# Attention and two MLPs on one core: more q/k and V-half buffers, V read once per batch, W1o staged in its own tile, W1i's low halves on VectorE

## The chip, the cores and the metric

One core of one Trainium2 chip. The time is the device time of one execution in microseconds (us). Engines are called as in the profile: PE is TensorE, DVE is VectorE, ACT is ScalarE, POOL is GpSimd, SP is SyncE, which issues all DMAs here.

## The reference

Inputs are q, k, v of shape (4 batches, 8 heads, 576 positions, 64), and four weight matrices: W1i and W2i (512 x 2048), W1o and W2o (2048 x 512). All are float32, except that the kernel receives the weights as 64-bit values seen as pairs of 32-bit words.

```
q_rot, k_rot = rotate(q), rotate(k)
scores = scale * q_rot @ k_rot.T
attn = exp(scores - max) / (sum + 1e-9)
x = (attn @ v) as (2304 tokens, 512)
x = gelu_sigmoid(x @ W1i) @ W1o
out = elu(x @ W2i) @ W2o
```

## The kernel before, in words

**Precision.** Every large matrix product is done in two 16-bit halves: an operand is scaled, rounded to a high half (f16), and the remainder is kept as a low half. Three products (high-high, high-low, low-high) are added in PSUM. So each operand costs one operation for its high half (mostly ACT) and one for its low half (mostly DVE).

**Blocks and groups.** The 2304 tokens are cut into nine blocks: batch 0 into three of 128, 192 and 256 tokens, each later batch into two of 320 and 256. The eight heads are taken as four pairs. The attention of one pair in one block is called a group here. `s_units` does it for each query chunk: score matmuls (L702), maximum (L707, DVE), exponential (L711, ACT), reciprocal of the sum (L718, L722), high and low half of the weights (L727 or L729, L733), and a DMA transpose into a buffer of the pool `et` (L742). A full chunk has two tiles of 128x576, one per head; the 64 tail positions of both heads share one tile. `av_unit` then does attention times V for the group (L770) and splits the result into an `x` buffer (L773, L777). A block with its four `x` buffers complete can go through the first MLP: `first_mlp` (L821 and L858 on PE, L824 to L839 on ACT and DVE). Blocks 0 and 1 share one activation buffer `ghl`; from block 2 on, the MLP of a block starts when the one before has ended.

**What must come first.** `prep` (L570) loads q and k of a pair into a buffer `R`, rotates them on DVE (L582, L586, L590) with a buffer `T`, turns them on PE (L595) and stores them in a buffer `qkT` (L600) that stays taken until the pair's last score matmul of the batch. `v_prep` (L628) loads V per pair with four DMAs (L638, L640) into one of four `V` buffers, takes its largest absolute value (L644 or L646), and when the batch's scale is known splits it into halves in `v16` (L665, L669), of which shifted copies are made by three DMAs (L674 to L676).

**Weights.** `Weight` (L375) loads W1i and W1o in 16 chunks of 512 KB each (L406) into raw buffers: for W1i four places in `ghl` (`G`), for W1o two buffers of their own (`Go`). A chunk is brought to float32 by L413 and L420 (ACT or DVE), L427 and L432 (DVE only), and measured by four small matmuls (L446). When all 16 are through and the scale is known, each chunk is split in place into its high half (L489 or L491) and its low half. The low half is normally DVE's (L495). For W1i's first 12 chunks (`pe_w1i=12`) it is PE's instead: two float32 products with a scaled unit matrix (L503) minus one with the high half (L504), and a copy out of PSUM (L509 on ACT or L511 on DVE). The scaled unit matrix (L479) and the negative one (`minus`, L562) are made on POOL.

**The order.** Nothing is issued in program order. `Plan.run` is a list scheduler that runs when the kernel is built: every operation has a cost for each engine that may take it, a key (lower goes first, from the table `TUNE`), the operations it comes after, and the buffers it needs from pools whose sizes stand in `BUFS`. An operation without a free buffer is passed over for the next by key. The order in which the plan takes operations is the order of each engine's instructions, SP's DMA issues among them; on the chip each engine then works through its list in that order.

```
        o1 = op({"pe": ...}, mm, qk_ready[b, hp], key - TUNE["s"], need=[("s", x) for x in hS], use=[hX])
...
            trs.append(op(*cost, lambda e, a=a: tr(e, a), [o7] + trs[:1], key + a - TUNE["tr"], need=[("et", hT)] if fst else (), use=[hEl[a]] + ([] if fst else [hT])))
```

So a group takes its `et` buffer, of which there are two, at its first transpose and gives it back after its L770.

Of the kernel before, what the change touches and what calls it, by code (L numbers as in the profile page):

```python
# [20 lines left out]
    s=2, av=1, m=3, E=3, Ehl=3, et=2, qkT=2, R=1, V=4, T=2, v16=3, x=9, t=3, y=1, R2=3, yhl=1, o=3,  # L21
)
TUNE = dict(
    pe_w1i=12, pe_w1o=0, tab=-297.6168609712772, f_dve=2174.208136010006, f_act=81.41105488268754, f_pool=1052.0627577352195,
    w1i2=233.92485834008724, w1o2=-15.505291206809591, dlat=823.3988909607715, kt=-377.2719573514129, slack=1000000000.0,
    w1i=-242.99841865529547, w1i_s=3.8061508400859974, w1o=2.969689623870087, w1o_s=0.2720231588088968, prep0_s=3.8536381936457946,
    prep0=17.464678152527306, prep=-308.1411248258243, va0=-34.247727670237225, va=-64.95846168300157, vs=243.43590834219214,
    tiny=52.0380520808221, av=136.85433893694528, ex=-71.59782834058082, mx=198.562005486859, s=130.46174549696988, tr=52.58804387596749,
    w2i2=-139.37012827254537, w2o2=-97.97140032540149,
# [190 lines left out]
def kernel(  # L220
# [88 lines left out]
    buf("V", ap_, [P, 640], F32, BUFS["V"])  # L309
    buf("T", ap_, [P, 9, 2, D], F32, BUFS["T"])  # L310
    buf("v16", ap_, [P, 2, 5, 2, D], F16, BUFS["v16"])
    buf("vsh", ap_, [P, 4, 2, D], F16, BUFS["v16"])
# [22 lines left out]
    def across(am, hM, after, key, add=False, use=()):  # L335
# [19 lines left out]
        o = op({"pe": 300.0}, turn, list(after) + [ready_c], key, need=[("m", hM)], use=use)  # L355
# [19 lines left out]
    class Weight:  # L375
        def __init__(self, tile_fn, src, wide, tag, rbuf, key, after=()):
# [20 lines left out]
            for i, c in enumerate(seq):  # L397
                kc = key(i)

                def load(e, c=c):  # L400
                    if wide:
                        kk, f = c // 4, c % 4
                        s = src[kk * P:kk * P + P, 1024 * f:1024 * f + 1024]
                    else:
                        s = src[c * P:c * P + P, :]
                    nc.sync.dma_start(out=take((tag, c))[:, 0:1024].bitcast(I32), in_=s)  # L406
# [28 lines left out]
                ld = op(*dma_in(P * 4096), load, after, kc, need=[(rbuf, h)])  # L435
                self.loads.append(ld)
                ox = op({"act": c_act(512) + 70, "dve": c_dve(512, 2)}, cx, [ld], kc, use=[h], port=True)
# [3 lines left out]
                if by_pe:  # L441
                    def norm(e, c=c, i=i):
                        y = take((tag, c))[:, 0:1024].bitcast(BF16).rearrange("p (f w) -> p f w", w=4)[:, :, 3]
# [32 lines left out]
            if TUNE.get("pe_" + tag, 0):  # L476
                def scaled_eye(e):
                    self.eye = ap_.tile([P, P], F32, name=tag + "_eye")
                    ENG[e].tensor_scalar(out=self.eye, in0=eye, scalar1=self.sc["s"], scalar2=1.0, op0=ALU.mult, op1=ALU.mult)  # L479

                oe = op({"dve": 200, "pool": 360}, scaled_eye, [so, ready_c], key(15), port=True)
            self.ready = [None] * 16
            free = {}
            for i, c in enumerate(seq):
# [13 lines left out]
                if i < TUNE.get("pe_" + tag, 0):  # L498
                    hm = (tag, "lo", c)

                    def mm(e, c=c, i=i, hm=hm):
                        ps = take(hm)
# [3 lines left out]
                    def lo_(e, c=c, hm=hm):  # L506
                        l = self.h[:, self.at[c], 512:1024]
                        if e == "act":
                            nc.scalar.activation(out=l, in_=take(hm), func=AF.Copy)  # L509
                        else:  # L510
                            nc.vector.tensor_copy(l, take(hm))  # L511

                    o3 = op({"pe": 1500.0}, mm, [o2, oe], ks, need=[("m", hm)])
                    self.ready[c] = free[i + SP] = op({"act": c_act(512, True), "dve": c_dve(512)}, lo_, [o3], ks, use=[hm])
                    continue
# [27 lines left out]
    minus = ap_.tile([P, P], F16, name="minus")  # L543
# [6 lines left out]
    buf("Go", ap_, [P, 1024], F32, 2)  # L550
# [10 lines left out]
    def consts(e):  # L561
        nc.gpsimd.tensor_scalar(out=minus, in0=eye, scalar1=-1.0, scalar2=1.0, op0=ALU.mult, op1=ALU.mult)  # L562

    lit = op({"pool": 100}, light, key=-200.0)
    begin = op({"dma": 480}, 1600.0, start, key=TUNE["tab"])
    ready_c = op({"pool": 400}, consts, [begin], key=TUNE["tab"])


    def prep(b, hp):
# [41 lines left out]
        for g in range(3):  # L611
            t = op({"pe": 360.0}, lambda e, g=g: turn(e, g), [r3, ready_c, t], key, need=[("m", hX + (g,))] + ([] if g else [("qkT", hX)]), use=[hT] + ([hX] if g else []))
# [12 lines left out]
    v_loaded = {}  # L625
    def v_view(b, hp):
        return take(("vs", b, hp)).rearrange("p (a d) -> p a d", d=D)

    def v_prep(b):
        ka = first_u[fb[b], 0] - TUNE["va" if b else "va0"]  # L630
        ams = []
        for hp in range(NP):
            h, h0 = ("vs", b, hp), 2 * hp

            def ld_(e, h=h, h0=h0, hp=hp):
                t = v_view(b, hp)
                for a in range(2):
                    nc.sync.dma_start(out=t[:, a:8:2, 0:D], in_=v[b, h0 + a, 0:512, :].rearrange("(p j) d -> p j d", j=4))  # L638
                for a in range(2):
                    nc.sync.dma_start(out=t[64 * a:64 * a + 64, 8:10, 0:D], in_=v[b, h0:h0 + 2, 512:S, :].rearrange("h p d -> p h d"))  # L640

            def am(e, h=h, hp=hp):
                if e == "act":
                    nc.scalar.activation(out=junk.rearrange("p (a d) -> p a d", d=D), in_=v_view(b, hp)[:, :, 0:D], func=AF.Abs, saturate=False, accum_out=v_am[b % 2][:, hp:hp + 1])  # L644
                else:
                    nc.vector.tensor_reduce(out=v_am[b % 2][:, hp:hp + 1], in_=v_view(b, hp)[:, :, 0:D], axis=AX.XY, op=ALU.max, apply_absolute_value=True)  # L646

            ld = v_loaded[b, hp] = op(*dma_in(330e3, 4), ld_, [], ka + hp, need=[("V", h)])
# [11 lines left out]
        for hp in range(NP):  # L660
            ks = last_u[fb[b], hp] - TUNE["vs"]
            h, hv, hw = ("vs", b, hp), ("v16", b, hp), ("vsh", b, hp)

            def hi(e, hp=hp, hv=hv):
                nc.scalar.activation(out=take(hv)[:, 0].rearrange("p j h d -> p (j h) d"), in_=v_view(b, hp)[:, :, 0:D], func=AF.Copy, scale=sc["s"])  # L665

            def lo(e, hp=hp, hv=hv):
                X = take(hv).rearrange("p w j h d -> p w (j h) d")
                nc.vector.scalar_tensor_tensor(out=X[:, 1], in0=v_view(b, hp)[:, :, 0:D], scalar=sc["s"], in1=X[:, 0], op0=ALU.mult, op1=ALU.subtract)  # L669
            o1 = op({"act": c_act(640, ptr=1)}, hi, [so], ks, need=[("v16", hv)], use=[h])  # L670
# [617 lines left out]
```

## Time and profile before

| | |
|---|---|
| median of 3 runs | 1058.03 us (1056.73 to 1059.0) |
| the profiled execution | 1058.17 us, span 1056.4 us |
| PE busy | 978.3 us (93%) |
| DVE busy | 858.2 us (81%) |
| ACT busy | 608.0 us (58%) |
| mean granted PE clock | 0.982 |
| PE busy, tenths, by fortieths of the span | 2578689999999999999999999999989999999997 |

The span runs from the first to the last instruction. The last line shows PE nearly always busy except in the first six fortieths, about 26 us each. A busy PE need not be at its full rate: the granted clock tells at which of two levels it ran (1.0 is 2.4 GHz, 0.5 is 1.2 GHz).

### The profile page before, as it was taken

The numbers are of one execution on the slowest core, as the hardware profiler recorded it, in microseconds if no ns is written. First come the engines' busy times: TensorE is split into PE (matmuls) and PEld (weight loads), VectorE is DVE, ScalarE is ACT, GpSimd is POOL, SyncE is SP. The second block draws the span as 40 slices with busy tenths as digits, with TensorE's granted clock in tenths as the row PEclk, the third lists the DMA queues.
The fourth block names the chain that finished last, engine by engine and source line by source line (L and its number), as shares of the span: only waits on it lengthen the run. The fifth ranks groups of instructions, "written<-read, shape, count | busy, mean of one in ns | idle before, by whom it ended". The sixth has DMA issues, their size and how long they took to land. (4 is left out here: it accounts for less than half of the span.)

```text
span 1056.4 us, 20058 instructions
## 1 busy us (share of the span) xinstructions
PE 978.3 (93%) x7790; PEld 686.8 (65%) x7790; DVE 858.2 (81%) x1688; ACT 608.0 (58%) x1167; POOL 1.7 (0%) x8
## 2 busy tenths in 40 slices
PE   2578689999999999999999999999989999999997
PEld 1234468877766667866678778744435855855886
DVE  6988899789788779786574979899999579579474
ACT  4767789547577658566563648476355145145151
POOL 0000000000000000000000000000000000000000
PEclk9989889999999999999999999999999999999999
DMA  8889966677767786672773442620000100100100
GB/s 305 235 191 196 210 119 110 125 132 141 132 145 124 128 131 128 108 126 24 130 127 119 156 143 89 199 81 1 20 21 20 46 16 3 63 16 9 38 16 20
DMA packets 233086, 109.45 MB, mean 104 GB/s; under 512 B 203040, under 2 KB 222112, under 8 KB 232992
## 3 DMA queue, kind: packets, MB, share of 16 engines
q1 hardware_dynamic: 232992, 108.18, 47.0%
q8 instruction: 61, 1.00, 0.4%
q14 instruction: 33, 0.27, 0.1%
HBM read 53.61 MB, written 9.44 MB: 60 GB/s over the span
## 5 line engine op out<-in xcount | busy, mean ns | idle before, releaser
L821 PE MATMUL m<-x,wi 128*128 128x256 f16 (+3 forms) x1728 | 198.0, 273 | 0.5 <-DVE t L827 0.5
L858 PE MATMUL m<-ghl,wo 128*128 128x256 f16 (+3 forms) x1728 | 197.5, 273 | 0.0
L1053 PE MATMUL m<-yhl,w2i 128*128 128x512 f16 (+1 forms) x960 | 190.2, 360 | 4.4 <-DVE e L1064 4.2
L858 PEld LDWEIGHTS <-wo 128*128 128x128 f16 x1728 | 155.9, 98 | 41.5 <-issue 12.4
L821 PEld LDWEIGHTS <-wi 128*128 128x128 f16 x1728 | 155.7, 98 | 41.8 <-issue 12.5
L1053 PEld LDWEIGHTS <-w2i 128*128 128x128 f16 x960 | 94.3, 98 | 98.2 <-issue 7.4
L733 DVE SCALAR_TENSOR_TENSOR Ehl<-E,st,Ehl 128x576 f16<-128x576 f32 x144 | 116.3, 811 | 26.7 <-ACT Ehl L727 25.7
L711 ACT ACTIVATE E<-s,st 128x576 f32<-128x576 f32 x144 | 106.1, 738 | 49.3 <-DVE st L707 28.9
L702 PE MATMUL s<-qkT 64*128 64x288 f32 (+1 forms) x640 | 116.1, 466 | 10.0 <-ACT E L711 9.9
L727 ACT ACTIVATE Ehl<-E,st 128x576 f16<-128x576 f32 x117 | 89.3, 769 | 54.1 <-DMA et<-Ehl 38.3
L707 DVE TENSOR_REDUCE st<-s 128x1 f32<-128x576 f32 x144 | 107.0, 750 | 11.6 <-PE s L702 11.3
L1056 ACT ACTIVATE e<-m,y_c 128x512 f32<-128x512 f32 (+1 forms) x80 | 50.7, 638 | 72.9 <-issue 48.7
L702 PEld LDWEIGHTS s<-qkT 64*128 64x128 f32 (+1 forms) x640 | 60.3, 191 | 42.1 <-ACT E L711 17.2
L1129 PEld LDWEIGHTS <-g 128*128 128x128 f16 x714 | 70.3, 99 | 9.5 <-issue 0.7
L824 ACT ACTIVATE t<-m,hsc 128x320 f32<-128x320 f32 (+3 forms) x96 | 55.4, 577 | 25.1 <-PE m L821 23.2
L1149 DVE SCALAR_TENSOR_TENSOR x<-z,eo,x 128x256 f32<-128x256 f32 x49 | 23.3, 482 | 49.6 <-PE z L1129 49.3
L827 DVE SCALAR_TENSOR_TENSOR t<-t,m 128x320 f32<-128x320 f32 (+3 forms) x96 | 52.4, 547 | 10.6 <-ACT t L824 10.2
L836 ACT ACTIVATE ghl<-t 128x320 f16<-128x320 f32 (+3 forms) x96 | 49.8, 520 | 15.6 <-DVE t L827 15.1
L1129 PE MATMUL z<-wo,g 128*128 128x256 f16 x504 | 58.0, 277 | 0.0
L1064 DVE SCALAR_TENSOR_TENSOR e<-m,y_c,e 128x512 f32<-128x512 f32 (+1 forms) x80 | 55.0, 690 | 0.4
L839 DVE SCALAR_TENSOR_TENSOR ghl<-t,ghl 128x320 f16<-128x320 f32 (+3 forms) x96 | 52.5, 549 | 3.3 <-ACT ghl L836 3.0
L770 PE MATMUL av<-et,v 128*64 128x256 f16 (+3 forms) x720 | 50.9, 290 | 3.5 <-DMA et<-Ehl 3.5
(164 smaller groups left out, 1241.0 us busy)
## 6 DMA issues: line engine op xcount, KB each, us to landing
ghl<-in_moe_w_in_dram SPq DMA_DIRECT2D x16, 512.0 KB, 6.7
Go<-in_moe_w_out_dram SPq DMA_DIRECT2D x16, 512.0 KB, 4.3
R<-in_moe_w_in_dram SPq DMA_DIRECT2D x16, 512.0 KB, 4.1
R<-in_moe_w_out_dram SPq DMA_DIRECT2D x16, 512.0 KB, 3.7
R<-in_k_dram SPq DMA_DIRECT2D x16, 256.0 KB, 2.9
R<-in_q_dram SPq DMA_DIRECT2D x16, 256.0 KB, 3.6
V<-in_v_dram SPq DMA_DIRECT2D x32, 128.0 KB, 2.9
R<-y_d SPq DMA_DIRECT2D x8, 512.0 KB, 4.3
```

The source lines that it names most:

```text
L702: nc.tensor.matmul(o, X[r, t:t + (TAIL if h is None else P)], X[r, NS * w:NS * w + NS], start=True, stop=True)
L707: nc.vector.tensor_reduce(out=st["t"][:, a:a + 1], in_=take(hS[a])[:, :, 0:NS], axis=AX.XY, op=ALU.max, negate=True)
L711: nc.scalar.activation(out=take(hE[a]).rearrange("p (c f) -> p c f", c=2), in_=take(hS[a])[:, :, 0:NS], func=AF.Exp, bias=t[:, a:a + 1], s ...
L727: nc.scalar.activation(out=X16[:, 0:S], in_=take(hE[a]), func=AF.Copy, scale=r)
L733: nc.vector.scalar_tensor_tensor(out=X16[:, S:2 * S], in0=E, scalar=r, in1=X16[:, 0:S], op0=ALU.mult, op1=ALU.subtract)
L821: nc.tensor.matmul(ps, W1i.lhs(kk, u, wl), x[:, xl, 0:N], start=kk == 0 and i == 0, stop=kk == KD - 1 and i == 2)
L824: nc.scalar.activation(out=flat(ht), in_=flat(hM), func=AF.Tanh, scale=hsc[b][:, 1:2])
L839: nc.vector.scalar_tensor_tensor(out=g_of(gl), in0=t_of(), scalar=DOWN / 2, in1=g_of(gh), op0=ALU.mult, op1=ALU.subtract)
L858: nc.tensor.matmul(ps[:, 0:N], W1o.lhs(f, d, wl), (gh, gl)[xl][:, f, g0:g0 + N], start=f == 0 and i == 0, stop=f == KF - 1 and i == 2)
L1053: nc.tensor.matmul(ps[:, 0:n], W2i.lhs(kk, u, wl), Y[:, xl, kk, 0:n], start=kk == 0 and i == 0, stop=kk == KD - 1 and i == 2)
L1064: nc.vector.scalar_tensor_tensor(out=t[:, 0:n], in0=take(hM)[:, 0:n], scalar=st["c"][:, 0:1], in1=t[:, 0:n], op0=ALU.mult, op1=ALU.max)
L1129: nc.tensor.matmul(ps, AT[A](p, gi, P * tt), BT[B](p, wl), start=p == 0 and i == 0, stop=p == 7 and i == 2)
```

## The change

- Pools: `qkT` 2 to 4, `R` 1 to 2, `T` 2 to 1, `v16` (with `vsh`) 3 to 4, `x` 9 to 10, `V` from four buffers of one pair to one buffer of the whole batch.
- V of a batch is loaded by three DMAs and kept by head, so each pair's half is one contiguous piece; the halves and the shifted copies follow that layout.
- W1o's raw chunks lie in the part of W1o's own tile that is not yet written: chunks 0 to 7 in four places, 8 to 11 in two, 12 and 13 in one, 14 and 15 in the buffers `R`. Where a chunk's result falls on a place that held another raw chunk, it waits for that one (`over`).
- The PE way of making low halves is taken out, with `minus` and the scaled unit matrix: all W1i low halves are made by L495.
- A group's `et` buffer is taken by its first score matmul instead of its first transpose; the group's later score matmuls come after the first.
- All keys in `TUNE` are other numbers.

```
 BUFS = dict(
-    s=2, av=1, m=3, E=3, Ehl=3, et=2, qkT=2, R=1, V=4, T=2, v16=3, x=9, t=3, y=1, R2=3, yhl=1, o=3,
+    s=2, av=1, m=3, E=3, Ehl=3, et=2, qkT=4, R=2, V=1, T=1, v16=4, x=10, t=3, y=1, R2=3, yhl=1, o=3,
 )
...
-    pe_w1i=12, pe_w1o=0, tab=-297.6168609712772, f_dve=2174.208136010006, f_act=81.41105488268754, f_pool=1052.0627577352195,
...
+    tab=-755.3495038560459, f_dve=3717.3294571158176, f_act=658.9801078794787, f_pool=2518.1827925442094, w1i2=409.947966353374,
+    w1o2=-286.50084735922803, dlat=823.3988909607715, kt=40.753958365620065, slack=1000000000.0, w1i=-646.8295163812928,
...
+            stage = rbuf if callable(rbuf) else lambda c: rbuf
+            if callable(rbuf):
+                for k in range(4):
+                    buf(f"{tag}{k}", lambda i, k=k: self.t[:, 9 + 2 * k:11 + 2 * k, :].rearrange("p a b -> p (a b)"), None, None, 1)
...
+                over = []
+                if callable(rbuf) and c > 7:
+                    x = (4, 5, 10, 13)[(c - 8) // 2]
+                    over = [conv[x], am_ops[x]]
+                ox = op({"act": c_act(512) + 70, "dve": c_dve(512, 2)}, cx, [ld] + over, kc, use=[h], port=True)
...
-                if i < TUNE.get("pe_" + tag, 0):
-                    hm = (tag, "lo", c)
...
-                        nc.tensor.matmul(ps, self.eye, self.t[:, i + SP, :], start=True, stop=False)
-                        nc.tensor.matmul(ps, minus, self.h[:, self.at[c], 0:512], start=False, stop=True)
...
+        def ld_(e):
+            t = take(h)
+            nc.sync.dma_start(out=t[:, :, 0:4, :], in_=v[b, :, 0:512, :].rearrange("h (p j) d -> p h j d", j=4))
+            for a in range(2):
+                nc.sync.dma_start(out=t[64 * a:64 * a + 64, :, 4, :], in_=v[b, :, 512:S, :].rearrange("h p d -> p h d"))
+
+        ld = op(*dma_in(1311e3, 3), ld_, [], ka, need=[("V", h)])
...
-                nc.sync.dma_start(out=Y[0:64], in_=X[64:P, 0, 0:4])
-                nc.sync.dma_start(out=Y[64:P], in_=X[0:64, 0, 1:5])
-                nc.sync.dma_start(out=X[64:P, :, 4], in_=X[0:64, :, 0])
+                nc.sync.dma_start(out=Y[0:64], in_=X[64:P, 0, :, 0:4])
+                nc.sync.dma_start(out=Y[64:P], in_=X[0:64, 0, :, 1:5])
+                nc.sync.dma_start(out=X[64:P, :, :, 4], in_=X[0:64, :, :, 0])
...
-        o1 = op({"pe": 1260.0 if h is not None else 800.0}, mm, qk_ready[b, hp], key - TUNE["s"], need=[("s", x) for x in hS], use=[hX])
+        o1 = op({"pe": 1260.0 if h is not None else 800.0}, mm, qk_ready[b, hp] + first[:1], key - TUNE["s"], need=[("s", x) for x in hS] + ([("et", hT)] if i == first_u[n, hp] else []), use=[hX] + ([] if i == first_u[n, hp] else [hT]))
+        first.append(o1)
...
-    W1o = Weight(lambda: per.tile([P, 16 + SP, 512], F32, tag="wo", name="wo"), w1_out, False, "w1o", "Go", lambda c: TUNE["w1o"] + TUNE["w1o_s"] * c)
+    W1o = Weight(lambda: per.tile([P, 16 + SP, 512], F32, tag="wo", name="wo"), w1_out, False, "w1o", lambda c: f"w1o{c % 4 if c < 8 else 2 + c % 2 if c < 12 else 3}" if c < 14 else "R", lambda c: TUNE["w1o"] + TUNE["w1o_s"] * c)
```

## Rows read from the trace of the kernel before

**Rows 1.** Stretches of the span: span part, busy time (instructions) of each engine.
```profile
core 0: us, PE busy (x) PEld busy (x) DVE busy (x) ACT busy (x) POOL busy (x), PEclk, DMA share, GB/s
7.00:144.00 137.00, 86.31 (x610) 50.31 (x610) 123.61 (x243) 98.42 (x195) 0.93 (x1) 0.90 0.91 221
144.00:231.00 87.00, 82.50 (x1036) 71.42 (x1036) 77.95 (x147) 62.35 (x138) 0.00 (x0) 1.00 0.65 114
231.00:303.00 72.00, 71.22 (x648) 54.71 (x646) 61.69 (x118) 47.20 (x99) 0.00 (x0) 1.00 0.79 148
480.00:567.00 87.00, 86.59 (x761) 64.64 (x760) 53.05 (x101) 49.28 (x100) 0.00 (x0) 1.00 0.47 79
```

**Rows 2.** Timeline of PE: start, duration, instructions.
```profile
68.95 1.28 PE L770 MATMUL av<-et,v 128*64 128x128 f16 x20
...
144.14 1.81 PE L821 MATMUL m<-x,wi 128*128 128x128 f16 x24
...
183.66 1.24 PE L702 MATMUL s<-qkT 64*128 64x288 f32 x8
...
185.92 1.28 PE L770 MATMUL av<-et,v 128*64 128x256 f16 x20
...
230.86 4.10 PE L821 MATMUL m<-x,wi 128*128 128x256 f16 x36
```

**Rows 3.** Groups of PE's instructions from 0 to 231 us, by form.
```profile
L702 PE MATMUL s<-qkT 64*128 64x288 f32 x184 | 42.1, 532 | 3.9 <-ACT E L711 3.9
L503 PE MATMUL m<-wi,w1i_eye 128*128 128x512 f32 x24 | 14.4, 685 | 1.1 <-ACT qkT L600 1.1
L595 PE MATMUL m<-eye,T 128*128 128x128 f32 x63 | 12.7, 334 | 7.7 <-DVE T L590 4.7 <-ACT qkT L600 1.4 <-DVE t L827 1.1
L702 PE MATMUL s<-qkT 64*64 64x288 f32 x56 | 11.3, 536 | 5.7 <-ACT E L711 5.6
L770 PE MATMUL av<-et,v 128*64 128x256 f16 x100 | 7.2, 287 | 1.5 <-DMA et<-Ehl 1.5
L504 PE MATMUL m<-wi,minus 128*128 128x512 f16 x12 | 5.0, 412 | 5.3 <-ACT wi L489 5.3
L770 PE MATMUL av<-et,v 128*64 128x320 f16 x20 | 1.5, 301 | 0.0
```

**Rows 4.** Groups of DVE's instructions from 0 to 231 us.
```profile
L733 DVE SCALAR_TENSOR_TENSOR Ehl<-E,st,Ehl 128x576 f16<-128x576 f32 x49 | 39.5, 809 | 5.2 <-ACT Ehl L727 5.1
L707 DVE TENSOR_REDUCE st<-s 128x1 f32<-128x576 f32 x52 | 38.9, 748 | 3.2 <-PE s L702 3.1
L582 DVE TENSOR_TENSOR T<-R,tab 128x576 f32<-128x576 f32 x16 | 12.0, 750 | 1.0 <-DMA R<-in_q_dram 0.7 <-issue 0.2
L495 DVE SCALAR_TENSOR_TENSOR wo<-wo,w1o_s 128x512 f16<-128x512 f32 x16 | 11.8, 736 | 0.0
L590 DVE TENSOR_TENSOR T<-T,R 128x1152 f32<-128x1152 f32 x8 | 10.8, 1349 | 0.0
L586 DVE TENSOR_TENSOR R<-R,tab 128x1152 f32<-128x1152 f32 x8 | 10.8, 1345 | 0.0
L669 DVE SCALAR_TENSOR_TENSOR v<-V,v_s,v 128x640 f16<-128x640 f32 x8 | 6.8, 876 | 0.0
```

**Rows 5.** Timeline of DVE: two L733 in a row.
```profile
66.53 1.54 DVE L733 SCALAR_TENSOR_TENSOR Ehl<-E,st,Ehl 128x576 f16<-128x576 f32 x2
```

**Rows 6.** Waits of PE from 0 to 250 us: total, times, longest.
```profile
PE m L446 <- DVE ghl L427: 21.2, 11, 8.1
```

**Rows 7.** Timeline of SP's queue: two DMA issues for V.
```profile
43.30 2.61 SPq L640 DMA_DIRECT2D V<-in_v_dram  x2
```

**Rows 8.** DMA issues of the whole span: count, size, median us to landing.
```profile
Go<-in_moe_w_out_dram SPq DMA_DIRECT2D x16, 512.0 KB, 4.3
V<-in_v_dram SPq DMA_DIRECT2D x32, 32.0 KB, 2.6
v<-v SPq DMA_DIRECT2D x16, 32.0 KB, 1.9
```

More of the change, by code (lines that the diff above doesn't have):

```diff
@@ L353, in back @@
             nc.tensor.matmul(take(hM)[:, 256:257], square[0:1], st["r"][0:1], start=True, stop=True)
-        o = op({"pe": 300.0}, turn, list(after) + [ready_c], key, need=[("m", hM)], use=use)
+        o = op({"pe": 300.0}, turn, list(after) + [begin], key, need=[("m", hM)], use=use)
         o = op({"dve": 220.0}, most, [o], key, use=[hM])
@@ L405, in load @@
                         s = src[c * P:c * P + P, :]
-                    nc.sync.dma_start(out=take((tag, c))[:, 0:1024].bitcast(I32), in_=s)
+                    first()
+                    nc.sync.dma_start(out=flat(c).bitcast(I32), in_=s)
                 def cx(e, c=c, i=i):
@@ L434, in __init__ @@
                 h = (tag, c)
-                ld = op(*dma_in(P * 4096), load, after, kc, need=[(rbuf, h)])
+                ld = op(*dma_in(P * 4096), load, after, kc, need=[(stage(c), h)])
                 self.loads.append(ld)
-                ox = op({"act": c_act(512) + 70, "dve": c_dve(512, 2)}, cx, [ld], kc, use=[h], port=True)
+                over = []
[3 more added lines that the diff above has]
+                ox = op({"act": c_act(512) + 70, "dve": c_dve(512, 2)}, cx, [ld] + over, kc, use=[h], port=True)
                 orr = op({"act": c_act(512) + 60, "dve": c_dve(512, 2)}, cr, [ld], kc, use=[h], port=True)
@@ L475, in __init__ @@
             self.raw_done = conv
[L476 to L481, printed above, removed]
             self.ready = [None] * 16
@@ L611, in prep @@
         for g in range(3):
-            t = op({"pe": 360.0}, lambda e, g=g: turn(e, g), [r3, ready_c, t], key, need=[("m", hX + (g,))] + ([] if g else [("qkT", hX)]), use=[hT] + ([hX] if g else []))
+            t = op({"pe": 360.0}, lambda e, g=g: turn(e, g), [r3, begin, t], key, need=[("m", hX + (g,))] + ([] if g else [("qkT", hX)]), use=[hT] + ([hX] if g else []))
             out.append(op({"act": c_act(384, True)}, lambda e, g=g: put(e, g), [t], key - TUNE["kt"], use=[hX + (g,), hX]))
@@ L624 @@
     v_scaled = {}
-    v_loaded = {}
     def v_view(b, hp):
-        return take(("vs", b, hp)).rearrange("p (a d) -> p a d", d=D)
+        return take(("vs", b))[:, 2 * hp:2 * hp + 2].rearrange("p h j d -> p (h j d)")
     def v_prep(b):
@@ L681, with s_units @@
     x_ready = {}
-    def s_units(i, trs):
+    def s_units(i, trs, first):
         n, hp, j, h = units[i]
@@ L755, in s_units @@
             o7 = op({"dve": c_dve(S, ptr=1)}, lambda e, a=a: lo(e, a), [o6], key + a, use=[hE[a], hEl[a]], port=True)
-            fst = i == first_u[n, hp] and not a
-            trs.append(op(*cost, lambda e, a=a: tr(e, a), [o7] + trs[:1], key + a - TUNE["tr"], need=[("et", hT)] if fst else (), use=[hEl[a]] + ([] if fst else [hT])))
+            trs.append(op(*cost, lambda e, a=a: tr(e, a), [o7], key + a - TUNE["tr"], use=[hEl[a], hT]))
     av_done = {}
@@ L769, in mm @@
                 for a in range(2):
-                    nc.tensor.matmul(ps[64 * a:64 * a + 64, 0:N], W[:, j, a, :] if w == 2 else V[:, w, j, a, :], T[:, a, blk, 0:N], start=i == 0, stop=i == len(slots) - 1)
+                    nc.tensor.matmul(ps[64 * a:64 * a + 64, 0:N], W[:, a, j, :] if w == 2 else V[:, w, a, j, :], T[:, a, blk, 0:N], start=i == 0, stop=i == len(slots) - 1)
         def hi(e):
@@ L1217 @@
         for hp in range(NP):
-            trs = []
+            trs, first = [], []
             for i in range(first_u[n, hp], last_u[n, hp] + 1):
                 if units[i][3] != 1:
-                    s_units(i, trs)
+                    s_units(i, trs, first)
             av_unit(n, hp, trs)
```

66 lines of the change are left out of this document (24 added, 42 removed).

## The prediction, made before the changed kernel was built or run

> **What bounds the kernel now.** I read the page first, then the span cut into stretches, then the timeline of TensorE (PE), its groups and VectorE's (DVE) in the early part. In the stretches [rows 1] PE is busy 95% from 144 us, 99% from 231 on, but only 86.3 of the 137.0 us from 7 to 144. What PE lacks there is its large work: the first MLP opens with block 0 at 144.14 us and reaches block 2 at 230.86 [rows 2]. Before that it lives on scores, small measuring matmuls (in their gaps alone it waits 21.2 us for DVE [rows 6]) and W1i's low halves, 14.4 + 5.0 = 19.4 us [rows 3]. DVE in the same 137 us is busy 123.6, or 90%: it sets the pace of everything PE waits for. So the early stage is bound by DVE and by the order in which DVE's work is spent; the rest is bound by PE.
>
> Why block 0 waits until 144: with two q/k buffers, pairs 0 and 1 must finish all three blocks of batch 0 before pairs 2 and 3 can begin, so block 0 is complete only when nearly all of batch 0 is. With four buffers, pairs 0 to 3 can do block 0 first.
>
> **The balance.** I count to D, the first matmul of block 2. In both kernels the same must lie before D: W1i and W1o whole (block 1's second product needs all of W1o, and block 2 follows block 1), batch 0's attention, the MLPs of blocks 0 and 1. After D PE runs at 99% [rows 1]. So the gain is the distance by which D comes earlier, less the work of batch 1 that the old kernel had done by then.
>
> PE's batch 1 work before 231: 240 score matmuls [rows 3] less batch 0's 160 leaves 80, ten units at 1.24 us [rows 2], 12.4; attention times V of one 320-token group 2.2 (1.5 for twenty of 28 matmuls) and one 256-token group 2.0 (7.2 / 5 for twenty of 28); q/k turns of three pairs (63 matmuls are seven pairs, 12.7 us) about 5. Sum 21.5. So D's old place is worth 230.9 - 21.5 = 209.4 us. **A new D before 209.4 is a gain, one after it a loss.**
>
> The new D, from DVE: it was busy 123.6 + 78.0 = 201.6 us from 7 to 231 [rows 1]. An instruction right behind another costs less than its duration: two L733 take 1.54, not 1.62 [rows 5], so I take 0.08 off each. Batch 1's share in it [rows 4]: 16 maxima (52 less 36) at 0.67 = 10.7; 13 low halves (49 less 36) at 0.73 = 9.5; the rotation of four pairs, 8 x 0.67 + 4 x 1.27 + 4 x 1.27 = 15.5; four V low halves at 0.80 = 3.2; reciprocals, V maxima and x about 3. Sum 42. That leaves 159.6. The change adds twelve W1i low halves at 0.66 = 7.9, less two copies out of PSUM that DVE made, about 1.2: 166. Density: 90% as from 7 to 144, or 100% at best. Some of the 10% are waits that two q/k buffers and two W1o buffers cause; I take 92%, near the measured one since the mix is the same. D = 7 + 166 / 0.92 = 187. Gain 209.4 - 187.4 = 22 us.
>
> The profiled execution took 1058.17 us, against a median of 1058.03, so one stands for the other: 1058 - 22 = **1036**.
>
> **Does the gain stay?** Behind D the old kernel had 42 us of batch 1 done on DVE, the new one none. Block 2's MLP with block 3's attention is about 73 us of PE; DVE needs for it the 15.5 of rotation, twenty tiles at about 1.55 = 31, V 5, and block 2's activations about 12, some 65. That fits without slack; 61.7 of 72 is what it did in that stretch before [rows 1]. Later there is slack: from 480 to 567 DVE is busy 53.1 of 87 [rows 1], since attention has run two blocks ahead and waits for x buffers. A gain over some 40 us would use this up; 22 does not.
>
> **The parts, one by one.**
> - *W1i's low halves.* PE loses 19.4 us, but before 144, where it has 51 idle: nothing by itself. DVE's 6.7 us count in full, they are in the sum above. ScalarE loses ten evictions, not its bound.
> - *V whole.* Per batch 16 DMA issues become three. Two cost up to 2.61 us of SP's queue [rows 7], with transposes queued behind them. Three at that price are 4 us. The gain lies in SP, which is ahead of DVE most of the time: nought to 3 us, taken as nothing. New is that V of a batch cannot load before the one before is split; with four halves the split is early, and the next V is wanted only at D: nothing.
> - *V's shifted copies.* The same bytes in runs half as long. The nearest rows are the 1.9 us of such a copy and the 2.6 of a V tail with short runs [rows 8]: nought to 0.7 us once, ahead of the first attention times V; taken as nothing.
> - *W1o staged in its tile.* Four places, then two, then one. At the narrow end chunks 8, 10, 12 and 13 follow one another, each 4.3 us of load [rows 8] and about 3 of conversion: some 30 us for eight chunks, where the old kernel spread 16 over more than 100. Nothing; up to 10 us if they start late.
> - *T 2 to 1, R 1 to 2.* DVE's rotation of a pair waits for PE to turn the one before (about 1.5 us), while q/k come earlier. Minus 1 to plus 4 us over four pairs, DVE has weights to convert meanwhile: nothing.
> - *et taken at the first score matmul.* This is the wait that the change adds; see the slower rival.
> - *x 9 to 10, POOL's two matrices gone, the moved keys:* off the path; the keys act only through the order, which is what the density and the rivals cover.
>
> **Two rules.** PE in the stretch 7 to 144 had a mean granted clock of 0.90, against 1.00 once it was 95% busy [rows 1]. The Trainium skill, page "TensorE: Matmul & The Clock Gate", section "Why this matters for your kernels", says that idle gaps between bursts of matmuls put the clock back to half rate; this speaks against taking 36 filler matmuls out of a stretch with gaps. By it the time is the clock rival's below; by the rows of a fed PE it is the forecast. The Trainium skill, page "DMA: Bandwidth & Descriptors", section "Specifications", puts the least size for line rate at 512 B; by that the shifted copies, cut to 128 B pieces, would be slower, and the sum with the upper end above would be a microsecond longer.
>
> **The rivals.**
> 1. *Slower: et becomes the bound.* A group's scores now wait until the group two before has done its attention times V; behind the waiting score matmul on PE everything later in its list stands, and DVE's maxima starve. The old kernel, whose two buffers held back only transposes, spread its twelve batch 0 groups from 68.95 to 185.92 [rows 2], 10.6 us each. At that pace and start the new D is about 69 + 11 x 10.6 + 2 = 188, as DVE's sum gives; so the margin is thin. It decides at (209.4 - 71) / 11 = 12.6 us a group. At 13.3 D is 217: 1066. For it: DVE now has two stages of weights to convert between a group's steps. Against: a group needs only 3 to 6 us of DVE, and V arrives earlier than before.
> 2. *The clock.* Between the first MLP and D, PE has some 93 of work for 92 us. Had it a granted clock of 0.80 in this stretch instead of about 0.95, it would need some 14 us more, less what DVE leaves: 1048. For it: the 0.90 from 7 to 144, at lower PE load. Against: PE at 95% busy ran at 1.00 [rows 1].
> 3. *No change: block 0 stays late.* If the keys put W1o ahead of block 0's tiles, the first MLP opens near 130 instead of about 95, and the added DVE work and the better order cancel: 1058.
> 4. *More gain: DVE gapless.* At 97% D is 178: 1027; at 100% 173 and 1022, and 1019 with a few conversions on ScalarE. For it: DVE has more choices at any time (four q/k buffers, four W1o places).
>
> **How the numbers follow.** Forecast (density 88 to 94%: 1031 to 1045) 0.57; denser 0.13; clock 0.10; no change 0.06; slower 0.14. A measurement of this kernel can tell 0.2%, about 2 us. Faster is the forecast, denser and the clock: 0.80; same 0.06; slower 0.14. The range holds the first three, so 0.80: from 1019 to 1052, the clock case with the bounds of the V and W1o parts on it.
>
> **What would show it.** Right: no L503 and L504; the first L821 between 85 and 110 us instead of 144; block 2's first L821 near 187 instead of 231, with DVE about 92% busy until then; PE from there on as full as before, and the attention of the last block ending with block 6's first product again. The forecast is wrong if block 2 opens after 205; if the score matmuls wait for transposes and L770 by tens of us (rival 1); if the granted clock between the first MLP and D is under 0.85 (rival 2); or if PE shows new idle time after D, which would mean that DVE's lost lead is missed, above all where W2 is converted.

## The result and the profile after

The changed kernel takes 1040.73 us (median of 4, 1036.90 to 1041.09), the kernel before 1057.88 beside it: a ratio of 0.983, 95% interval 0.9804 to 0.9855. It is 17.2 us faster; 22 were forecast, and the time lies inside the range (1019 to 1052).

The page of the profile after, first its span and busy times, then PE's busy share and its granted clock by fortieths (tenths):

```profile
span 1039.2 us, 19888 instructions
PE 959.6 (92%) x7754; PEld 682.4 (66%) x7754; DVE 864.1 (83%) x1695; ACT 603.8 (58%) x1161; POOL 0.4 (0%) x6
PE   2447899999999999999999999999989999999997
PEclk8555899999999999999999999999999999999999
```

PE is busy 18.7 us less than before (978.3), nearly the 19.4 us of products that were taken out [rows 3]. It is tempting to take this removed work for the gain. Experiment 1 shows that it isn't: the same products taken out of the old kernel make it slower. Where the time went is seen when the span is cut at the two moments the forecast is about, the first MLP's opening and block 2's first matmul:

```profile
core 0: us, PE busy (x) PEld busy (x) DVE busy (x) ACT busy (x) POOL busy (x), PEclk, DMA share, GB/s
7.00:97.60 90.60, 41.89 (x324) 28.41 (x324) 83.37 (x148) 66.49 (x128) 0.00 (x0) 0.57 0.93 264
97.60:207.30 109.70, 101.94 (x1190) 84.68 (x1189) 104.26 (x211) 83.41 (x177) 0.00 (x0) 0.93 0.71 127
207.30:1039.20 831.90, 815.80 (x6245) 569.31 (x6242) 676.49 (x1339) 452.64 (x856) 0.00 (x0) 1.00 0.39 85
137.80:207.30 69.50, 67.77 (x808) 58.32 (x806) 66.63 (x119) 52.17 (x109) 0.00 (x0) 1.00 0.71 124
480.00:567.00 87.00, 87.00 (x780) 68.16 (x778) 55.40 (x100) 40.87 (x82) 0.00 (x0) 1.00 0.54 114
```

DVE is busy 92% up to the opening and 95% from there to block 2. PE is not half busy up to the opening, 93% from there, and from 137.8 on it has no time left (67.77 of 69.5). DVE is nearly as full there (66.63), but most of the batch 1 work that it does before block 2, and that block 2 doesn't need, lies in this stretch. So the bound passes from DVE to PE before block 2, and not at it. The timeline of PE gives the moments (start, duration, line, tile, matmuls in one run, idle time before it):

```profile
65.47 0.32 PE L757 MATMUL av<-et,v 128*64 128x128 f16 x1
67.99 2.29 PE L689 MATMUL s<-qkT 64*128 64x288 f32 x8
75.43 0.30 PE L462 MATMUL m<-ones,wo 128*128 128x1 bf16 x4 [5.15 <-DVE wo L439]
75.66 1.55 PE L757 MATMUL av<-et,v 128*64 128x128 f16 x20
77.57 2.29 PE L689 MATMUL s<-qkT 64*128 64x288 f32 x8
84.65 2.29 PE L689 MATMUL s<-qkT 64*128 64x288 f32 x8
95.39 2.29 PE L689 MATMUL s<-qkT 64*128 64x288 f32 x8
97.62 2.56 PE L808 MATMUL m<-x,wi 128*128 128x128 f16 x33
...
120.83 0.29 PE L462 MATMUL m<-ones,R 128*128 128x1 bf16 x4 [1.21 <-DVE R L439]
122.43 0.38 PE L346 MATMUL m<-eye,w1o_a 128*1 128x128 f32 x2
137.82 0.83 PE L845 MATMUL m<-ghl,wo 128*128 128x128 f16 x12
195.17 0.30 PE L757 MATMUL av<-et,v 128*64 128x256 f16 x1
207.27 2.78 PE L808 MATMUL m<-x,wi 128*128 128x256 f16 x24
280.83 3.42 PE L808 MATMUL m<-x,wi 128*128 128x320 f16 x24
```

The first MLP opens at 97.62 instead of 144.14 (L821 [rows 2]), block 2 at 207.27 instead of 230.86, block 3 at 280.83. In between stand two moments that the forecast has no term for: 122.43, when W1o's last chunk (in a buffer `R`, measured at 120.83) is through and its scale is made, and 137.82, block 0's second product. What leads up to them is seen in SP's timeline (the loads of W1o from the eighth chunk on), then in DVE's and PE's:

```profile
68.05 1.00 SPq L418 DMA_DIRECT2D wo<-in_moe_w_out_dram  x2
73.98 1.05 SPq L418 DMA_DIRECT2D R<-in_moe_w_out_dram  x2
81.15 1.01 SPq L418 DMA_DIRECT2D wo<-in_moe_w_out_dram  x2
94.42 0.35 SPq L418 DMA_DIRECT2D wo<-in_moe_w_out_dram  x1
106.00 0.33 SPq L418 DMA_DIRECT2D wo<-in_moe_w_out_dram  x1
...
130.67 0.74 DVE L505 SCALAR_TENSOR_TENSOR wi<-wi,w1i_s 128x512 f16<-128x512 f32 x1
133.55 0.74 DVE L505 SCALAR_TENSOR_TENSOR wo<-wo,w1o_s 128x512 f16<-128x512 f32 x1
...
131.47 0.23 PE L808 MATMUL m<-x,wi 128*128 128x128 f16 x1 [1.68 <-DVE wi L505]
```

The loads are those of chunks 8 and 9, 14 and 15 (into `R`), 10 and 11, 12, and 13. Each pair or chunk has to wait until the one before it has left its place, so they stand 13.1, 13.3 and 11.6 us apart, and from the last load to the scale it is 16.4: 54.4 us in all. Behind the scale DVE makes W1o's low halves among attention's work; the second product needs the first four, and the fourth is made at 133.55. W1i's last low half is made as late as 130.67, and PE waits for it at 131.47, still in block 0's first product.

### The profile page after: what moved, and what is told of

It reads as the page before. It is cut to its first block, busy times and chain, and to the rows that moved or that the text cites. A ratio compares the mean times of both kernels' runs of the same rounds, so it can differ in the third digit from the quotient of the medians.

```text
span 1039.2 us, 19888 instructions
## 1 busy us (share of the span) xinstructions
PE 959.6 (92%) x7754; PEld 682.4 (66%) x7754; DVE 864.1 (83%) x1695; ACT 603.8 (58%) x1161; POOL 0.4 (0%) x6
## 5 line engine op out<-in xcount | busy, mean ns | idle before, releaser
L808 PE MATMUL m<-x,wi 128*128 128x256 f16 (+3 forms) x1728 | 199.9, 275 | 2.1 <-DVE wi L505 1.7
L845 PE MATMUL m<-ghl,wo 128*128 128x256 f16 (+3 forms) x1728 | 198.2, 273 | 0.2 <-DVE wo L505 0.2
L808 PEld LDWEIGHTS <-wi 128*128 128x128 f16 x1728 | 157.6, 99 | 45.7 <-issue 14.7
L845 PEld LDWEIGHTS <-wo 128*128 128x128 f16 x1728 | 155.7, 98 | 41.7 <-issue 12.5
L698 ACT ACTIVATE E<-s,st 128x576 f32<-128x576 f32 x144 | 106.0, 737 | 67.8 <-DVE st L694 60.8
L689 PE MATMUL s<-qkT 64*128 64x288 f32 (+1 forms) x640 | 108.2, 459 | 4.1 <-ACT E L698 4.0
L714 ACT ACTIVATE Ehl<-E,st 128x576 f16<-128x576 f32 x105 | 79.9, 772 | 31.3 <-DMA et<-Ehl 10.1
L689 PEld LDWEIGHTS s<-qkT 64*128 64x128 f32 (+1 forms) x640 | 56.4, 189 | 33.1 <-issue 10.6
L1116 PEld LDWEIGHTS <-g 128*128 128x128 f16 x714 | 69.5, 98 | 8.7 <-issue 0.7
```

The source lines that it names most:

```text
L689: nc.tensor.matmul(o, X[r, t:t + (TAIL if h is None else P)], X[r, NS * w:NS * w + NS], start=True, stop=True)
L698: nc.scalar.activation(out=take(hE[a]).rearrange("p (c f) -> p c f", c=2), in_=take(hS[a])[:, :, 0:NS], func=AF.Exp, bias=t[:, a:a + 1], s ...
L714: nc.scalar.activation(out=X16[:, 0:S], in_=take(hE[a]), func=AF.Copy, scale=r)
L808: nc.tensor.matmul(ps, W1i.lhs(kk, u, wl), x[:, xl, 0:N], start=kk == 0 and i == 0, stop=kk == KD - 1 and i == 2)
L845: nc.tensor.matmul(ps[:, 0:N], W1o.lhs(f, d, wl), (gh, gl)[xl][:, f, g0:g0 + N], start=f == 0 and i == 0, stop=f == KF - 1 and i == 2)
L1116: nc.tensor.matmul(ps, AT[A](p, gi, P * tt), BT[B](p, wl), start=p == 0 and i == 0, stop=p == 7 and i == 2)
```

## The experiments

The table puts the four moments of every kernel side by side, each the start of a run in PE's timeline: first MLP (L808 in after), W1o's scale (L346 on `w1o_a`), block 0's second product (L845), block 2 (L808 with 256 tokens). The experiments below refer to it. Times are medians, and the ratios below are to the kernel before, which took 1057.3 to 1058.4 beside them. None is faster than the changed kernel. Each kernel is planned anew by the scheduler, so an edit also moves operations that it doesn't name.

| kernel | time, us | first MLP | W1o scale | second product | block 2 |
|---|---|---|---|---|---|
| before | 1057.9 | 144.1 | 143.6 | 162.3 | 230.9 |
| after | 1040.7 | 97.6 | 122.4 | 137.8 | 207.3 |
| 1 before, lows on DVE | 1065.4 | 154.6 | 143.7 | 176.6 | 241.0 |
| 2 after, lows on PE | 1053.3 | 98.1 | 119.1 | 139.1 | 216.1 |
| 3 after, two q/k buffers | 1070.4 | 147.9 | 131.4 | 162.7 | 246.4 |
| 4 after, filler on PE | 1064.8 | 114.2 | 142.1 | 158.3 | 228.7 |
| 5 two `et`, control | 1076.3 | 140.4 | 137.5 | 152.5 | 239.0 |
| 6 three `et` | 1074.7 | 130.2 | 155.2 | 173.7 | 251.5 |
| 7 after, old keys | 1059.0 | 110.2 | 130.6 | 144.2 | 229.0 |
| 8 after, W1o later | 1058.0 | 98.4 | 140.5 | 157.5 | 235.9 |
| 9 after, W1o earlier | 1049.3 | 97.8 | 122.8 | 135.9 | 213.1 |
| 10 before, new keys | 1063.8 | 144.4 | 157.0 | 175.3 | 247.1 |
| 11 after, three q/k buffers | 1053.6 | 140.1 | 124.1 | 155.2 | 230.1 |
| 12 after, one `R` | 1056.7 | 109.1 | 134.4 | 148.4 | 229.4 |

Down the table, block 0's second product comes 12 to 22 us after the later of the first two moments, and block 2 follows it by 64 to 87 us. In after it follows by 69.5, of which PE is busy 67.8. What the second product waits for can be said more closely: in eleven of the fourteen kernels it starts 0.1 to 4.8 us behind the end of DVE's fourth low half of W1o. In the other three (1, 3 and 11), where the first MLP opens 11 to 16 us behind the scale, it is 16 to 21 us.

**1. The old kernel, all W1i low halves on DVE.** Is it the order, or the work taken off PE?

```diff
-    pe_w1i=12, pe_w1o=0, tab=-297.6168609712772,
+    pe_w1i=0, pe_w1o=0, tab=-297.6168609712772,
```

> The kernel before with W1i's low halves all on VectorE (the 36 products on TensorE gone), nothing else changed. Theory (order): the 19.4 us of TensorE lie in its idle time before the first MLP, so taking them away only adds idle time, and VectorE's 6.7 us more come on top: 1058 to 1065 us, first MLP at 140 to 152 us. Rival (work): the changed kernel's TensorE is 18.7 us less busy and as idle as before, so the removed work is the gain: about 1039 us, and the rest of the change is worth nothing.

Measured: 1065.44 us, ratio 1.0072 [1.0053, 1.0090]: 7.1 slower. The page's busy times, some stretches, and the score matmuls' group of the whole span (busy, mean ns, idle), here and in the kernel before:

```profile
PE 977.5 (92%) x7754; PEld 689.9 (65%) x7754; DVE 862.5 (81%) x1696; ACT 605.3 (57%) x1164; POOL 0.7 (0%) x7
```

```profile
60.00:97.60 37.60, 22.74 (x179) 14.78 (x178) 33.95 (x62) 24.08 (x51) 0.00 (x0) 0.78 0.87 183
97.60:144.00 46.40, 32.01 (x213) 19.53 (x209) 43.34 (x87) 33.44 (x69) 0.00 (x0) 0.65 0.88 190
144.00:207.00 63.00, 57.62 (x733) 48.62 (x732) 54.69 (x108) 46.37 (x101) 0.00 (x0) 0.90 0.53 100
```

```profile
L702 PE MATMUL s<-qkT 64*128 64x288 f32 (+1 forms) x640 | 125.5, 485 | 11.5 <-ACT E L711 11.4
...
L702 PE MATMUL s<-qkT 64*128 64x288 f32 (+1 forms) x640 | 116.1, 466 | 10.0 <-ACT E L711 9.9
```

The rival is out, and the theory has the sign right: without the new order, the move costs time. Its size is at the theory's upper end (1065), near the 6.7 us that the move adds to DVE, but not shown to be made of them: the opening came at 154.6 (140 to 152 were expected) and block 2 at 241.0, both 10 us later than in before, and DVE's busy time rose by only 4.3. PE lost 19.4 us of products, yet is busy only 0.8 less. The score group alone shows how: 125.5 us against 116.1 in before, the same 640 matmuls, as the granted clock lay at 0.65 to 0.90 between 60 and 207. A sum of busy time mixes work with the rate at which it ran.

**2. The new kernel, twelve low halves on PE again.** The same question from the other side.

```diff
+    pe_w1i=12, pe_w1o=0,
...
+                        nc.tensor.matmul(ps, self.eye, self.t[:, i + SP, :], start=True, stop=False)
+                        nc.tensor.matmul(ps, minus, self.h[:, self.at[c], 0:512], start=False, stop=True)
```

> The changed kernel with the TensorE way of making W1i's first 12 low halves put back. Theory (order): most of these products fall before the first MLP at 97.6 us, where TensorE is idle for more than half of the time, and VectorE is relieved of 6.7 us: 1036 to 1050 us, most of the gain stays. Rival (work): 1058 us, the gain is gone.

Measured: 1053.33 us, ratio 0.9959 [0.9942, 0.9977]: 12.6 slower than after. This lies between the two expectations (1036 to 1050, and 1058): most of the gain is gone, but not all of it. From its timeline of PE:

```profile
76.21 1.24 PE L719 MATMUL s<-qkT 64*128 64x288 f32 x8
98.08 0.84 PE L838 MATMUL m<-x,wi 128*128 128x128 f16 x12
99.88 1.13 PE L520 MATMUL m<-wi,w1i_eye 128*128 128x512 f32 x2 [0.16 <-DVE v_m L368]
104.37 1.13 PE L520 MATMUL m<-wi,w1i_eye 128*128 128x512 f32 x2
108.22 1.08 PE L520 MATMUL m<-wi,w1i_eye 128*128 128x512 f32 x2
216.12 1.47 PE L838 MATMUL m<-x,wi 128*128 128x256 f16 x12
```

Two things follow. The first MLP opens at 98.08, as in after, though DVE had been spared nine low halves by then and PE ran at its full rate from 76 on (eight score matmuls in 1.24 us, in after 2.29 until 98): relieving both does not bring the opening forward. (The products for nine chunks, some 13.5 us of PE, stand before it; that they cost just what the relief gave is not excluded.) And three of the twelve products now come after the opening, where PE has little idle time to give (4.5 us of the 41 from 98 to 139): some 1.5 us each with the high half's (1.13 and 0.38), 4.5 together. The rest of the 12.6 is not assigned to anything; block 2 is 8.9 late, block 3 11.8.

With 1 and 2 the four corners are known: order old or new, lows on PE or DVE: 1058 and 1065, 1053 and 1041 (order here stands for the rest of the change: pools, V, W1o and keys). The order alone gives 5, the lows alone cost 7, both together give 17.

**3 and 11. Two and three q/k buffers in the new kernel.**

```diff
-    s=2, av=1, m=3, E=3, Ehl=3, et=2, qkT=4, R=2,
+    s=2, av=1, m=3, E=3, Ehl=3, et=2, qkT=2, R=2,
```

(and `qkT=3` in 11)

> The changed kernel with two q/k buffers instead of four. Theory (order): pairs 2 and 3 must wait for pairs 0 and 1 to end the batch again, the first MLP opens at 130 us or later and the gain is lost: 1055 us or more. Rival (work): the buffers do not matter, 1041 us within 5.

> The changed kernel with three q/k buffers. Pair 3 then waits for pair 0 to end batch 0. Theory: block 0 is late again by most of that, first MLP after 120 us, 1050 to 1070 us. Rival (two more buffers are not both needed): 1041 within 5.

Measured: with two 1070.38 us, ratio 1.0128 [1.0095, 1.0162]; with three 1053.55, 0.9958 [0.9933, 0.9982]. The first MLP moves back to 147.9 and 140.1, the old place, and W1o's scale stands ready 16 us before it in both. The theory holds in both: the early opening needs all four buffers, the third brings 8 us of it, the fourth 42. The opening is not the whole of the time, though: with three buffers it is back at 140, and 4 us of the gain are still there.

**7 and 10. The pools with the old keys, and the keys with the old pools.** In 7 the lines of `TUNE` from `tab` to `w2o2` are those of the kernel before, in 10 the other way round, with `pe_w1i=12` kept:

```diff
-    tab=-755.3495038560459, f_dve=3717.3294571158176, f_act=658.9801078794787, f_pool=2518.1827925442094, w1i2=409.947966353374,
...
+    tab=-297.6168609712772, f_dve=2174.208136010006, f_act=81.41105488268754, f_pool=1052.0627577352195,
...
```

> The changed kernel with the keys of the kernel before (pools, V, W1o and the low halves as in the changed kernel). Theory (the pools make the order): first MLP before 120 us, 1038 to 1052 us. Rival (the keys make it): first MLP near 144, 1058 us or more.

> The kernel before with the keys of the changed kernel, W1i's twelve low halves still on TensorE. Theory (keys and pools only work together): two q/k buffers keep block 0 late, first MLP at 135 us or later, 1056 to 1075 us. Rival (the keys carry the gain): 1050 us or less.

Measured: 1058.97 us, ratio 1.0008 [0.9995, 1.0021], and 1063.77, 1.0061 [1.0042, 1.0081]. The pools alone (with V, W1o and the low halves as in after) open the first MLP at 110.2, 34 us earlier than before, as was expected, but they gain nothing, where 6 to 20 us were expected: W1o's scale is at 130.6, block 2 at 229.0. The keys alone lose 6, as the theory of 10 has it. Only both together pay.

**8 and 9. W1o later and earlier.** One key, -94.9, becomes -60 in 8 and -130 in 9:

```diff
-    w1i_s=9.364510121035858, w1o=-94.86665171188625, w1o_s=9.112725926177722,
+    w1i_s=9.364510121035858, w1o=-60.0, w1o_s=9.112725926177722,
```

> The changed kernel with the key of W1o's loads and conversions raised from -94.9 to -60: about four chunks later in the order. If VectorE's work ahead of block 0 sets the opening of the first MLP, it opens 3 to 8 us earlier than 97.6. If the et wait sets it, it stays within 2 us. The time: 1036 to 1050 us, either way, as W1o is then wanted by the second product of block 0.

> The changed kernel with the key of W1o's loads and conversions lowered from -94.9 to -130, the other way from the run before it. There W1o's scale came at 140.5 us instead of 122.4, block 2 opened at 235.9 instead of 207.3, and the time was 17 us longer. Theory (W1o's end is the second thing that sets block 2, beside TensorE's own work): the scale comes before 118 us; block 2 opens within 5 us of 207, as from there TensorE's own 92 us of work after the first MLP's opening is the limit: 1035 to 1046 us. Rival (W1o alone sets it): block 2 opens 10 us or more earlier, 1031 us or less.

Measured: 1057.95 us, ratio 1.0007 [0.9990, 1.0024], and 1049.33, 0.9917 [0.9899, 0.9935]. PE's timeline of 8, then of 9:

```profile
98.38 2.17 PE L808 MATMUL m<-x,wi 128*128 128x128 f16 x36
140.54 0.38 PE L346 MATMUL m<-eye,w1o_a 128*1 128x128 f32 x2
157.46 0.83 PE L845 MATMUL m<-ghl,wo 128*128 128x128 f16 x12
235.87 1.48 PE L808 MATMUL m<-x,wi 128*128 128x256 f16 x12
```

```profile
97.79 2.85 PE L808 MATMUL m<-x,wi 128*128 128x128 f16 x48
122.76 0.38 PE L346 MATMUL m<-eye,w1o_a 128*1 128x128 f32 x2
213.11 2.78 PE L808 MATMUL m<-x,wi 128*128 128x256 f16 x24
```

Both times are missed, and together the two say most. In 8 the opening stays at 98, the scale moves by 18 us, the second product by 20, block 2 by 29, and the whole gain is gone: the opening is worth nothing unless W1o keeps pace. The second product starts 0.6 us behind DVE's fourth low half of W1o there, which ends at 156.84. In 9 a lower key doesn't bring the scale forward. The last three loads into W1o's own places stand at 81.17, 94.45 and 105.96, as in after (81.15, 94.42, 106.00): the chain of places holds the scale at 122, and not the key. What the key did move is the work on PE between the opening and the second product: 26.57 us of 38.10 in 9, against 34.17 of 40.20 in after (the stretches of both, 97.8 to 135.9 and 97.6 to 137.8). By an estimate some 5 of these 7.6 us are rate (the same 192 first products take 12.1 us in 9, 14.3 in after); the rest is work, eight score matmuls and one group's attention times V, which 9 does behind the second product instead. PE is idle 11.5 us there against 6.0, 6.7 of them for transposes (0.7 in after). From the second product to block 2 it then has 73.29 us to do, against 67.77, and block 2 opens 5.8 later; what makes up the rest of the 8.6 is open.

**12. One buffer `R`.** The last two chunks of W1o lie in `R`, as q and k do.

```diff
-    qkT=4, R=2, V=1, T=1,
+    qkT=4, R=1, V=1, T=1,
```

> The changed kernel with one R buffer instead of two. I priced the second R at nought to 1 us of gain for the q/k loads. Theory: 1040 to 1047 us. Rival (the last two W1o chunks, which pass through R, come one after the other and W1o ends later): W1o's scale after 128 us and 1047 to 1060 us.

Measured: 1056.70 us, ratio 0.9986 [0.9971, 1.0001]: 16 slower than after, as the rival has it. The scale moves to 134.4, the second product to 148.4, block 2 to 229.4. So `R` is one of the things that set W1o's end: with one of it chunks 14 and 15 go through the same buffer one after the other, between q and k (the last is loaded at 124.82, behind the conversion of the other at 123.31). The opening moves too, to 109.1, which fits q and k waiting for the buffer (the loads of batch 0's last pair start at 39.28, in after at 21.66), so the 16 us are not W1o's end alone.

**4. Filler on PE.** Five matmuls of 448 columns are added behind each of the 32 chunk norms; they compute nothing that is used. Does the low clock cost time?

```diff
+                        for m in range(5):
+                            nc.tensor.matmul(ps[:, 64:512], y[:, P * (m % 4):P * (m % 4) + P], y[:, 0:448], start=True, stop=True)
```

> The changed kernel with five useless bf16 products of 448 columns after each of the 32 measurements of a W1 chunk, to keep TensorE's clock up before the first MLP (granted 0.50 from 20 to 98 us in the changed kernel). If the low clock costs time there, the score and attention products before 98 us shorten by half (some 22 us of TensorE less) and the time falls by 3 to 10 us: 1031 to 1038. If TensorE only waits for VectorE there, the clock rises and the time stays: 1041 within 3, or some us longer where the filler stands in the way.

Measured: 1064.75 us, ratio 1.0064 [1.0049, 1.0079]: 24 slower than after, far from both expectations. Its stretches:

```profile
7.00:60.00 53.00, 42.53 (x196) 19.11 (x197) 45.16 (x70) 35.15 (x67) 0.00 (x0) 0.87 0.84 264
60.00:97.60 37.60, 31.65 (x180) 12.87 (x179) 24.73 (x51) 19.84 (x37) 0.00 (x0) 0.82 0.79 182
```

The clock rose (0.57 to 0.87 and 0.82; eight score matmuls at 35.29 take 1.31 us), but DVE fell to 24.73 of 37.6 us: what it needs from PE stood behind the filler. So this run says nothing on the clock by itself; experiment 2 does.

**5 and 6. Two and three `et` buffers.** So that a third fits, both have `qkT=3`, `R=1` and `x=8`:

```diff
-    E=3, Ehl=3, et=2, qkT=3, R=1, V=1, T=1, v16=4, x=8,
+    E=3, Ehl=3, et=3, qkT=3, R=1, V=1, T=1, v16=4, x=8,
```

> The changed kernel with three q/k buffers, one R and eight x buffers: the room that a third et buffer needs, without the third et buffer. Control for the next run. Both theories: 1040 to 1056 us, somewhat slower than the changed kernel, since pair 3 gets its q/k buffer later; first MLP between 97 and 110 us.

> The same with three et buffers. Theory (the et wait sets the pace up to the first MLP: in the changed kernel each new group's scores follow an attention product of the group two before, 9 to 10 us apart, and the first MLP opened at 97.6 with VectorE loaded and at 98.1 with it relieved of 7 us): the groups come closer, the first MLP opens 5 to 15 us before that of the control, and the time falls by 3 to 12 us below the control. Rival (VectorE at 92% sets it): first MLP within 3 us and time within 3 us of the control.

Measured: 1076.30 us, ratio 1.0180 [1.0161, 1.0199], and 1074.73, 1.0158 [1.0141, 1.0175]. The control itself came out far above what was expected, so the pair tells little: a third `et` opens the first MLP 10 us earlier (130.2 against 140.4), W1o's scale falls back by 18, and the intervals of the times overlap. In this kernel the wait for `et` delays the opening; what it costs in the changed kernel, and in the whole, stays open.

## Why the prediction was right, and where its sizes were off

**Right: the opening and the density.** "The first L821 between 85 and 110" was 97.62, "DVE about 92% busy" was 92% up to it. The products of L503 and L504 are gone. The reason given for it holds: experiments 3 and 11 undo it with the q/k buffers alone. The price of W1i's low halves, 6.7 us, lies near the 7.1 of experiment 1, but there PE's rate fell as well, so the nearness may be luck.

**Mis-sized: block 2 at 187.** It came at 207.3, so by its own criterion (after 205) that step failed. The forecast took D from DVE's sum. The sum itself was good: DVE was busy 187.6 us from 7 to 207.3, of which some 30 are batch 1's (44 maxima and 41 low halves of the attention's weights by then, 36 and 36 of them batch 0's; eight pairs rotated, four of them batch 1's, eight V halves), and 158 remain, against 166. But DVE's sum was no longer the bound: it had time for those 30 us. PE was, and W1o ahead of it. From the opening to block 2 PE has 101.94 us of work, 10.3 of it batch 1's (see below). The other 91.6, without a gap, put D at 189.2; the 7.8 us in which PE was idle put it at 197.0, and batch 1's work at 207.3. So in the forecast's own counting, which has no batch 1 work before D, block 2 came 9.6 us late (197.0 against 187.4). The forecast had PE's 93 us beside the sum, in its clock rival, and left no time for waits in them.

The term that failed is "W1o staged in its tile: nothing; up to 10 us if they start late". The narrow end of its places, "some 30 us" in the forecast, took 54 (68.05 to 122.43), since the loads landed in 5.8 us (median) instead of 4.3, and a conversion waits its turn on ACT and DVE: chunk 12, loaded at 94.42, was through at 105.9. From the second product to block 2 it is 69.5 us in after, 59.2 without batch 1's work; a D at 187.4 wants the second product at 128.2, and it came at 137.8, 9.6 us later and 15 us behind W1o's scale. Experiments 8 and 12 delay that scale by 18 and 12 us, and lose 17 and 16 us. How much an earlier W1o would give back is not shown: no run moved its scale forward by more than 3.4 us, and W1i's last low half, at 130.67, would then be the next to wait for.

The price of `R`, "nothing" in one line with `T`, belongs to the same step: `R` was counted as a buffer of q and k, though two chunks of W1o lie in it. By experiment 12 the second one is worth 16 us, for both uses together. (The forecast's density range of 88 to 94% works out at 1032 to 1044, for the 1031 to 1045 that it gives; nothing hangs on it.)

**Why it was 17 and not 2.** D moved only 23.6 us earlier, and by the forecast's own balance (old 209.4 after batch 1's work) that would give 2. But the new kernel too did some of batch 1's work before D, from 171 us on: by 207.3 PE had done 200 score matmuls, 40 more than batch 0's 160 (five units, 6.1 us), and 63 turns, three pairs of batch 1's among them (27 of them took 4.2 us). That is 10.3. That puts the new D at 197 and the gain at 12.4. The other 4.8 lie behind D: after has 11.2 us more to do there than before (21.5 - 10.3), and takes 6.4 longer (831.9 against 825.5 us). Idle time behind D is the same in both (16.1 and 15.9), so this is work that ran faster, and no new wait. Most of it is PE's rate, which the kernel before lost for a while in two places. The same matmuls there, then in after, from PE's timelines:

```profile
383.62 2.80 PE L770 MATMUL av<-et,v 128*64 128x320 f16 x20
386.20 1.18 PE L770 MATMUL av<-et,vsh 128*64 128x320 f16 x8
1038.07 9.69 PE L1129 MATMUL z<-wo,g 128*128 128x256 f16 x72
...
248.34 1.55 PE L757 MATMUL av<-et,v 128*64 128x320 f16 x20
249.72 0.71 PE L757 MATMUL av<-et,vsh 128*64 128x320 f16 x8
1022.50 8.02 PE L1116 MATMUL z<-wo,g 128*128 128x256 f16 x72
```

The first two together took 1.65 us longer in before, the third 1.67: 3.3 of the 4.8. The rest is not assigned to anything. The forecast has no such term. So the 17 us stand so near the 22 in part by luck: 9.6 were lost before D, and 4.8 came back behind it.

**Does the gain stay.** Yes, as forecast. From 480 to 567 PE is as full as before and DVE has nearly the same slack (55.40 of 87 busy, 53.05 before). The last attention times V ends at 549.4 instead of 566.4, 17 us earlier.

**The rivals.** *et:* the wait acts. Twelve batch 0 groups opened their attention times V from 65.47 to 195.17, 11.8 us each, slower than the old 10.6 [rows 2], and each new group's scores stand right behind one such run (67.99, 77.57, 84.65, 95.39 in the timeline). It stayed short of the 12.6 where it would decide. *No change* did not come about, since the opening was early; but that W1o's place in the plan can eat the whole gain is what experiment 8 shows (1058), with W1o too late and not too early. *Gapless DVE* fell with the bound. *The clock:* between the opening and block 2 it was 0.93, so the rival did not come about as a whole. Up to the second product it was 0.82, though, which is some 7 us of PE by an estimate (0.18 of 40.2); what they cost in time no run separates.

The clock did fall, in a place the forecast didn't name: 0.57 in the mean before the opening. The rule of the Trainium skill, page "TensorE: Matmul & The Clock Gate", section "Why this matters for your kernels", that gaps put the clock back to half rate, agrees with this and with experiment 1. What it would make of the time did not show before the opening: experiment 2 has the full rate there from 76 us on and opens no earlier.

The small copies between V's halves, of which the old ones took 1.9 us [rows 8], landed in 2.1. The Trainium skill, page "DMA: Bandwidth & Descriptors", section "Specifications", wants 512 B for line rate; the direction agrees. It doesn't single the rule out, since the 64 KB copies, whose runs were cut from 1024 to 512 B and so still meet it, went from 2.1 to 2.3 us as well. The sum holds without it.

**Open.** What holds the opening at 97.6 is not settled. It is not W1o's key (98.4 and 97.8 in 8 and 9), and taking the low halves off DVE with PE at full rate did not move it (98.1 in 2). The pace of the `et` buffers, with norms of W1o's chunks in PE's list between the groups (the 5.15 us at 75.43), would fit; in this kernel it was only read, and a third `et` was tested only in the slower kernel of 5. The longest step of it stands at the start: the third group's scores (67.99) come 33 us after the second's (34.58), right behind the first group's attention times V. Nor was it tried to give W1o's last two chunks buffers of their own; the memory that it takes was not looked for.

## What to carry to other kernels

A milestone has a bound for each engine and for each tensor that must be whole by then; work out all of them, and take the latest. Here the sum of the busiest engine gave a time 10 us too early, counted without the next batch's work, since a weight that had to be whole by then had been given no time of its own. A chain of staging places is one of these bounds: count its steps with the waits that the conversions have in their engines' lists. Freed work, more buffers and a new order can each be worth nothing or less alone and 17 us together, so undo them one by one and in pairs before any of them gets the credit.

## What the hardware did that was not expected

- In experiment 1 19.4 us of matmuls were removed and PE's busy time fell by 0.8, since the rest took longer, at a lower granted clock (0.65 from 97.6 to 144; the score matmuls alone took 9.4 us more).
- Before the opening half the rate cost the changed kernel nothing that could be found: the opening was at 97.6 with the clock at 0.57, and at 98.1 in experiment 2 with full rate from 76 on (and the products for nine chunks more on PE).
- A granted clock of 1.00 at the start of a trace is not always the rate. Experiment 2 lists 1.00 from 7 to 60 us, yet eight score matmuls at 34.00 take 2.29 us there, as they do in after at 34.58, where the page lists 0.5; at full rate they take 1.24. The kernel before does the same (2.29 at 21.30). So the 0.90 that the forecast read for the early stretch [rows 1] was too high: the duration of a known instruction is the surer sign. The mean over a whole execution can mislead in the same way: two executions of the changed kernel list 0.954 and 0.985 and took 1040.95 and 1041.09 us.
